# Early sums: stores and loads begun by ScalarE, three sum buffers, two weight buffers

## The chip, the cores and the metric

One core of one Trainium2 chip. The metric is device time in microseconds of one execution; three executions of the kernel before are known.

## The reference

Three layers follow each other. First a recurrence over 768 steps with a 40x40 state per head (4 batches of 8 heads). Its output is reshaped to 3072 tokens of 320 features. Then two feed-forward layers:

```
y[t] = r[t] @ state;  state = state * w[t] - (state @ a[t]) b[t]^T + v[t] k[t]^T
h = x @ w_in;  solu = h * softmax(h);  x = (layernorm(solu) * g_ln) @ w_out     # d_ff 1024
h = x @ w_in2; g = max(h, 0) + alpha * min(h, 0);  out = g @ w_out2             # d_ff 2048
```

## The kernel before

**Windows and slots.** The recurrence is cut into 12 windows of 64 steps; each window has two slots, so 24 slots, 0 to 23, run one after the other in `slot(g)`. A slot does the attention of 32 steps (`stage_x`, `stage_u`, `stage_uf`, `stage_st`, `stage_g2`, `stage_s`, `stage_y`) and, in between, pieces of work that lie in `queue`. Four slots share one triangular inverse (`inverse`, lines 368 and 372, 31 steps of VectorE), which is computed in the last two of the four slots before. TensorE runs in the order in which the program was written (`manual_schedule`). The other engines' instructions are put in order by the compiler's scheduler, by what it takes to be ready, and each engine then runs its own list strictly in order. SP (SyncE) begins all transfers, also strictly in order.

**The pieces in the queue.** `mlp_tasks(g)` fills it, in this order: the second transpose `ptx` of one token tile, then 16 products `mm1` of the first layer (line 589) with the transposes `ptr` (line 628) of another tile between them, then `soft` (the softmax pieces, lines 594 to 603, on VectorE, ScalarE and GpSimd), then the 8 steps of the second product `po` (lines 642 to 644). Normalising is line 606 on ScalarE. The tile for window w of the second layer's input is stored to `x2d` at line 663. `pace` and `wait` take pieces out of the queue to keep TensorE at work.

**The early sums.** The last layer's first product has 16 pieces f per window. For windows 1 to 8 the first 8 of them are computed ahead, in slots 9 to 23, as 64 units. A unit is four calls of `ahead_sums` (line 881, eight products of 128x256 in all) into the PSUM tile `ph1`. Then ScalarE copies the sum into the SBUF tile `hb` (line 884) and SP stores it to `hd` (line 886). It needs the weights `wr`, loaded from `whd` by `unit_load` (line 865) at the beginning of the unit two before, and the window's input `xw`, loaded by `window_load` (line 870) at the beginning of the window's first slot. Slots 9 to 22 have four units each, put after products 3, 7 and 16 and at the end of the queue; slot 23 has eight, the last five at the end of the queue.

**Buffers.** `hb` has one buffer, `xw` one, `wr` three. `ph1`, `ptr`, `po` and `ptx` share two PSUM buffers (pool `ps_w`).

**Other names that the steps touch.** VectorE's `lnl` (line 634) follows ScalarE's `lnh` (line 633) and frees `ptr`. `kbf` (line 244) and `XS` (line 254) are inputs of later windows, loaded by SP; GpSimd works on `XS` at line 326 and on `VUS` at line 499. Weights of the last layer are decoded from 64-bit words in the same slots (`raw`, `em`). After slot 23 a second phase does the last layer; there `hd` is read back.

Of the kernel before, what the change touches and what calls it, by code (L numbers as in the profile page):

```python
# [7 lines left out]
F32 = mybir.dt.float32  # L8
# [31 lines left out]
NI = 18  # L40
ZF = (1, 1, 1, 1)
WO, JW = 1, 2
NF, NR = 8, 3
UP = (3, 7, 16)
NH = 3
WF, WL = 1, 8
FLOOR2 = (4000, 1300)
U0 = 2 * WF + 7
# [6 lines left out]
def tile_kernel(ctx: ExitStack, tc: tile.TileContext, w_fm, a0_fm, a_fm, kb_fm, r_fm, v_fm, v_tm,  # L55
                w1_in, w1_out, g_ln, w2_in, w2_out, alpha, ident_d, mask_d, r, k, v, w, a, b, w1_nat, out,
                manual=True):
    nc = tc.nc
    NW = w_fm.shape[0]
    NG = 2 * NW  # L60
# [7 lines left out]
    def pool(stack, name, bufs, **kw):  # L68
        return stack.enter_context(tc.tile_pool(name=name, bufs=bufs, **kw))
# [13 lines left out]
    x2_d = [dr.tile([128, 5, 256], F32R, name=f"x2d{w}") for w in range(NW)]  # L83
# [5 lines left out]
    whd = [dr.tile([128, 2, 2, 3, 128], F32, name=f"whd{j}") for j in range(NF // 2)]  # L89
    hd = [[dr.tile([128, 512], F32, name=f"hd{w}_{f}") for f in range(NF)] for w in range(WF, WL + 1, 2)]  # L90

    cm = pool(ctx, "cm", 1)
    pm = ctx.enter_context(ExitStack())
    ps_h = pool(pm, "ps_h", 1, space=PSUM)
    ps_w = pool(pm, "ps_w", 2, space=PSUM)
    m1 = pool(pm, "m1", 1)
    m2 = pool(pm, "m2", 2)
    m3 = pool(pm, "m3", NR)
    b2 = pool(ctx, "b2", 2, side="right")
    lm = pool(ctx, "lm", 1, side="right")  # L100
    pa = ctx.enter_context(ExitStack())
# [25 lines left out]
    def f32(ap):  # L127
        return ap.bitcast(F32)
# [37 lines left out]
    st = {}  # L166
# [60 lines left out]
    def flush(n):  # L227
        while len(queue) > n:
            pop()
# [375 lines left out]
    def norm(P, m):  # L605
        nc.scalar.activation(out=P, in_=P, func=AF.Identity, scale=m[:, 8:9], bias=m[:, 9:10])
# [225 lines left out]
    def mlp_tasks(g):  # L832
        t1, t2 = g - 3, g - 4
        pt = PTR if g % 4 else PT0
        q = []
        us = slot_units(g)
        if 0 <= t2 - 1 < NG:
            q.append((0.33, 768, lambda: tr2(t2 - 1)))
        for p in range(17):
            if p == NP and 0 <= t2 < NG:  # L840
                q.append((0.0, 0, lambda: norm(st["P", t2], st["sm", t2])))
            if 0 <= t2 < NG:
                q += [(0.22, 512, lambda j=j: tr1(t2, j)) for j in range(4) if pt[j] == p]
            if 0 <= t1 < NG and p < 16:
                q.append((0.216, 512, lambda p=p: mm1(t1, p)))
            if p in UP and us:
                q += unit_tasks(us.pop(0))
        if 0 <= t1 < NG:
            q.append((0.0, 0, lambda: soft(t1)))
        if 0 <= t2 < NG:  # L850
            for p in range(K1):
                q.append((0.4, 960, lambda p=p: mm2(t2, p)))
        for i in us:
            q += unit_tasks(i)
        return q
# [2 lines left out]
    units = [(w, f) for w in range(WF, WL + 1) for f in range(NF)]  # L858
    loaded = []

    def unit_load():
        if len(loaded) < len(units):
            w, f = units[len(loaded)]
            t = m3.tile([128, 2, 3, 128], F32R, name="wr")
            nc.sync.dma_start(out=f32(t[:]), in_=whd[f // 2][:, f % 2])
            loaded.append(t)

    def window_load(w):
        st["xw"] = m1.tile([128, 5, 256], F32R, name="xw")
        nc.sync.dma_start(out=f32(st["xw"][:]), in_=f32(x2_d[w][:]))  # L870

    def ahead_sums(i, piece):
        w, f = units[i]
        if piece == 0:
            unit_load()
            st["ph"] = ps_w.tile([128, 512], F32, name="ph1", tag="w")[:, 0:256]
        wr, x, p = loaded[i], st["xw"], st["ph"]
        ops = [(wr[:, 0, 0], x[:, 0]), (wr[:, 0, 0], x[:, 1]), (wr[:, 1, 0], x[:, 0]), (wr[:, 0, 1], x[:, 2]),
               (wr[:, 0, 1], x[:, 3]), (wr[:, 1, 1], x[:, 2]), (wr[:, 0, 2], x[:, 4]), (wr[:, 1, 2], x[:, 4])]
        for j in range(2 * piece, 2 * piece + 2):  # L880
            nc.tensor.matmul(p, lhsT=ops[j][0], rhs=ops[j][1], start=j == 0, stop=j == 7)  # L881
        if piece == 3:
            hb = m1.tile([128, 256], F32, name="hb")
            nc.scalar.copy(out=hb, in_=p)  # L884
            c = (w - WF) % 2 * 256
            nc.sync.dma_start(out=hd[(w - WF) // 2][f][:, c:c + 256], in_=hb)

    def unit_tasks(i):
        return [(0.236, 512, lambda p=p: ahead_sums(i, p)) for p in range(4)]

    def slot_units(g):

        w, c = divmod(g - 7, 2)
        if not WF <= w <= WL:
            return []
        b = (w - WF) * NF
        if g == NG - 1:
            return list(range(b, b + NF))
        return list(range(b + c * NF // 2, b + (c + 1) * NF // 2))
# [22 lines left out]
    def slot(g):  # L922
        st["slot"] = g
        pre, late, at = fill_tasks(g)
        inv = inv_tasks(g)
        fin = g == NG - 1
        ni = len(inv)
        pos = [0]
        queue.extend(mlp_tasks(g))

        def dec(n=1):
            with tc.issue_after(st["fence"].ins):
                for _ in range(min(n, len(wts))):
                    wts.pop(0)()

        if g == NG - 2:
            at.setdefault("x", []).append(early_w)

        def filler(x):
            for f in at.get(x, ()):  # L940
                f()

        def invs(x):
            while pos[0] < ni and pos[0] < x * ni:
                inv[pos[0]]()
                pos[0] += 1

        if g + 1 < NG:
            load_g(g + 1)
        us = slot_units(g)  # L950
        if us and us[0] % NF == 0:
            window_load(WF + us[0] // NF)
            if us[0] == 0:
                for _ in range(NR - 1):
                    unit_load()
        stage_x(g)
        filler("a")
        with tc.issue_after(st["fence"].ins):
            for f in pre:
                f()  # L960
        filler("b")
        if g == 0:
            st["busy"] = st["idle"]
            keep(KEEP1)
        stage_u(g)
        nd = (ND if g < 4 else NL if g >= NG - 4 else NC)[g % 4]
        invs(0.2)
        stage_uf(g, 0)
        stage_uf(g, 1)
        filler("c")  # L970
        dec((nd + 3) // 4)
        invs(0.4)
        if not fin:
            stage_st(g, 0)
            stage_st(g, 1)
        invs(0.6)
        stage_g2(g, 0)
        dec((nd + 1) // 4)
        filler("x")
        filler("d")  # L980
        stage_g2(g, 1)
        invs(1.0)
        with tc.issue_after(st["fence"].ins):
            for f in late:
                f()
        filler("e")
        dec((nd + 2) // 4)
        if not fin:
            stage_s(g, 0)
            stage_s(g, 1)  # L990
        invs(1.0)
        dec(nd // 4)
        filler("f")
        flush(RES)
        stage_y(g)
        filler("z")
        flush(0)
        if g % 2 == 1 and not fin:
            x_move(g // 2)
# [462 lines left out]
```

## Time and profile before

| | |
|---|---|
| median of 3 executions | 1253.87 us (1252.38 to 1257.45) |
| profiled execution, its own time | 1249.18 us |
| span in the profile | 1247.4 us |
| mean granted TensorE clock | 0.879 |
| busy: TensorE / VectorE / ScalarE / GpSimd | 81% / 64% / 44% / 40% |
| slots 9 to 23 | about 390 to 917 us of the span |

In the rows, PE is TensorE's products and PEld its weight loads, DVE is VectorE, ACT ScalarE, POOL GpSimd, SP SyncE, and "SPq" SP's queue, which begins transfers. L884 is line 884 of the kernel. Times are microseconds from the start of the span, unless ns is said. A row of waits reads: engine, its line, whom it waited for, total us, times, longest. In rows in order of time, the bracket at the end tells how long the engine was idle before and what ended that. The issue of a transfer is not its movement: a row of SPq lasts as long as SP needs to begin it. PEclk is the granted clock as a share of 2.4 GHz. Idle time of an engine that isn't the bottleneck costs nothing.

### The profile page before, as it was taken

What the parts mean: (1) busy time and instruction counts of PE and PEld (TensorE: products, weight loads), DVE (VectorE), ACT (ScalarE), POOL (GpSimd) and SP (SyncE); (2) the same over time, 40 slices, a digit from 0 to 9 for tenths busy, and PEclk for the clock granted to TensorE, in tenths of its full rate; (3) what the DMA queues carried; (4) which work ended last, traced back from release to release, by engine and by line L of the source; (5) the groups of instructions that cost most, each with busy time, mean ns of one, the idle gap of its engine ahead of it and who ended that gap; (6) DMA issues with size and microseconds to landing.
All of it is one profiled execution on the core that took longest, in us unless ns stands there. A gap on an engine that the chain in (4) does not pass through costs nothing.

```text
span 1247.4 us, 38106 instructions
## 1 busy us (share of the span) xinstructions
PE 1008.0 (81%) x16197; PEld 841.3 (67%) x16197; DVE 794.3 (64%) x1610; ACT 544.3 (44%) x1268; POOL 501.3 (40%) x552
## 2 busy tenths in 40 slices
PE   7286676847786959697786877897888999999997
PEld 3144454736675757575675766776778999999997
DVE  8896899766985796467964686344346544444343
ACT  3335544555545625465454634554445322222221
POOL 6857545434353314233242322232215444444332
PEclk8586887778887978898788988998999999999999
DMA  6423343344444535464445555465374332330000
GB/s 169 121 63 99 97 116 101 103 115 115 111 129 128 165 99 155 146 181 136 127 129 164 144 165 153 137 205 172 118 214 165 92 105 58 108 115 30 22 19 17
DMA packets 139910, 149.93 MB, mean 120 GB/s; under 512 B 41428, under 2 KB 106580, under 8 KB 139732
## 3 DMA queue, kind: packets, MB, share of 16 engines
q1 hardware_dynamic: 139732, 147.42, 41.0%
q8 instruction: 129, 2.11, 0.7%
q14 instruction: 49, 0.40, 0.1%
HBM read 111.99 MB, written 35.39 MB: 118 GB/s over the span
## 4 chain that ended last, share of the span: by engine, by line
PE 40%; DVE 31%; DMA 9%; ACT 7%; issue 6%; POOL 5%; SPq 1%; POOLq 0%; DVEq 0%; ACTq 0%
PE ph L1126 9%; DVE tmp L368 6%; DVE LMN L372 5%; PE acc L1141 4%; PE acc L1139 4%; PE acc L1140 4%; PE h L589 3%; PE ph L881 2%; DVE VUS L496 2%; DMA raw<-in_w_in_dram 2%; DMA hd<-hb 2%; DMA kbf<-in_kb_fm_dram 2%; PE po L642 1%; DVE sm L594 1%; DVE kbf L317 1%
## 5 line engine op out<-in xcount | busy, mean ns | idle before, releaser
L1115 POOL TENSOR_TENSOR gll<-gt,gh 128x512 fp32r<-128x512 f32 (+1 forms) x112 | 126.9, 1144 | 174.1 <-ACT gh L1114 164.3
L1114 ACT CAST gh<-gt 128x512 fp32r<-128x512 f32 (+1 forms) x112 | 62.1, 560 | 199.8 <-DVE gt L610 188.1
L609 DVE TENSOR_SCALAR gt<-ph,al 128x512 f32<-128x512 f32 (+1 forms) x80 | 51.4, 643 | 145.4 <-PE ph L1126 145.2
L642 PE MATMUL po<-wo1h,lnh 128*128 128x320 f32 x192 | 73.1, 381 | 52.4 <-ACT hb L884 36.0
L881 PE MATMUL ph<-xw,wr 128*128 128x256 f32 x512 | 86.9, 302 | 22.5 <-DMA xw<-x2d 9.9
L589 PE MATMUL h<-w1h,xt 128*128 128x512 f32 x240 | 98.0, 461 | 0.0
L881 PEld LDWEIGHTS ph<-xw,wr 128*128 128x128 f32 x512 | 73.0, 197 | 33.1 <-issue 8.9
L368 DVE TENSOR_TENSOR tmp<-LMN,LMN 128x87 f32<-128x87 f32 (+25 forms) x189 | 90.1, 488 | 4.3
L1141 PE MATMUL acc<-w2h,gll 128*128 128x320 f32 x288 | 89.2, 310 | 0.0
L1139 PE MATMUL acc<-w2h,gh 128*128 128x320 f32 x288 | 89.1, 309 | 0.0
L1140 PE MATMUL acc<-w2l,gh 128*128 128x320 f32 x288 | 89.1, 309 | 0.0
L326 POOL TENSOR_TENSOR XS<-XS,H 40x512 f32<-40x512 f32 (+1 forms) x48 | 64.1, 1340 | 61.9 <-DMA XS<-in_a_fm_dram 34.0
L542 POOL TENSOR_TENSOR YS<-YS,mask 64x512 f32<-64x512 f32 x48 | 65.8, 1372 | 52.4 <-ACT YS L541 50.6
L225 PE MATMUL busy<-busy 128*128 128x512 bf16 x221 | 69.0, 469 | 20.0 <-DVE busy L1029 18.7
L642 PEld LDWEIGHTS po<-wo1h,lnh 128*128 128x128 f32 x192 | 43.3, 225 | 56.9 <-ACT hb L884 37.5
L679 POOL TENSOR_TENSOR dec<-em 128x256 f32<-128x256 f32 x36 | 28.7, 796 | 116.9 <-DVE em L676 73.5
L372 DVE TENSOR_TENSOR LMN<-LMN,tmp 128x87 f32<-128x87 f32 (+25 forms) x189 | 72.3, 394 | 3.4
L643 PE MATMUL po<-wo1l,lnh 128*128 128x320 f32 x192 | 67.2, 350 | 0.0
L644 PE MATMUL po<-wo1h,lnl 128*128 128x320 f32 x192 | 67.0, 349 | 0.0
L602 POOL TENSOR_TENSOR sm<-sm,half 128x1 f32<-128x1 f32 x24 | 15.6, 649 | 125.4 <-DVE sm L601 123.5
L589 PE MATMUL h<-w1l,xt 128*128 128x512 f32 x144 | 65.3, 454 | 0.0
L496 DVE TENSOR_TENSOR VUS<-pst,VUS 40x320 f32<-40x320 f32 x92 | 44.9, 488 | 29.4 <-PE pst L491 27.4
(205 smaller groups left out, 2816.7 us busy)
## 6 DMA issues: line engine op xcount, KB each, us to landing
wr<-whd SPq DMA_DIRECT2D x64, 384.0 KB
kbf<-in_kb_fm_dram SPq DMA_DIRECT2D x24, 416.0 KB
hd<-hb SPq DMA_DIRECT2D x64, 128.0 KB
hl<-hd SPq DMA_DIRECT2D x32, 256.0 KB
x2d<-x SPq DMA_DIRECT2D x24, 320.0 KB
xd<-Y SPq DMA_DIRECT2D x24, 256.0 KB
xt<-xd SPq DMA_DIRECT2D x12, 512.0 KB
raw<-in_w_in_dram SPq DMA_DIRECT2D x20, 256.0 KB
```

Source lines behind the costliest of these rows:

```text
L225: nc.tensor.matmul(st["busy"], lhsT=busy[:, 0:128], rhs=busy, start=True, stop=True)
L368: eng.tensor_tensor(out=tv[:, a - rows[0][0]:b - rows[0][0]], in0=M[:, a:b, s:s + 1].to_broadcast(sh), in1=l.unsqueeze(1).to_broadcast(sh) ...
L372: r = eng.tensor_tensor(out=o, in0=o, in1=tv[:, a - rows[0][0]:b - rows[0][0]], op=ALU.add)
L496: st["fence"] = nc.vector.tensor_tensor(out=d, in0=p_[o:o + 40], in1=v[o:o + 40, e, sl, :], op=ALU.add)
L589: nc.tensor.matmul(st["h"][:, ns], lhsT=l, rhs=r, start=j == 0, stop=j == len(ops) - 1)
L642: nc.tensor.matmul(po, lhsT=lh[:, k], rhs=wo1h[:, k], start=k == 0, stop=False)
L881: nc.tensor.matmul(p, lhsT=ops[j][0], rhs=ops[j][1], start=j == 0, stop=j == 7)
L1115: nc.gpsimd.tensor_tensor(out=gll, in0=t, in1=f32(gh), op=ALU.subtract)
L1126: nc.tensor.matmul(p, lhsT=l, rhs=r, start=j == 0, stop=j == len(ops) - 1)
L1139: nc.tensor.matmul(acc, lhsT=gh[:, cs], rhs=oh, start=first, stop=False)
L1140: nc.tensor.matmul(acc, lhsT=gh[:, cs], rhs=ol, start=False, stop=False)
L1141: nc.tensor.matmul(acc, lhsT=gll[:, cs], rhs=oh, start=False, stop=last)
```

## The change

ScalarE, not SP, begins the store of a sum, right behind its copy, then the load of the weights for the unit two later, and behind a window's last unit the load of the next window's input. `hb` gets three buffers (pool `mb`), `wr` two instead of three. The first window and the first two weight loads stay on SP, at the beginning of slot 9 (U0). In slot 23 the units go after products 1, 3, 5, 7, 10, 13 and 16, and one stays at the end.

```
-NF, NR = 8, 3
-UP = (3, 7, 16)
+NF, NR, NB = 8, 2, 3
+UP, UPL = (3, 7, 16), (1, 3, 5, 7, 10, 13, 16)
...
+    mb = pool(pm, "mb", NB)
...
-            if p in UP and us:
+            if p in (UP if g < NG - 1 else UPL) and us:
                 q += unit_tasks(us.pop(0))
...
-    def unit_load():
+    def unit_load(eng):
...
-            nc.sync.dma_start(out=f32(t[:]), in_=whd[f // 2][:, f % 2])
+            eng.dma_start(out=f32(t[:]), in_=whd[f // 2][:, f % 2])
             loaded.append(t)
 
-    def window_load(w):
+    def window_load(w, eng):
         st["xw"] = m1.tile([128, 5, 256], F32R, name="xw")
-        nc.sync.dma_start(out=f32(st["xw"][:]), in_=f32(x2_d[w][:]))
+        eng.dma_start(out=f32(st["xw"][:]), in_=f32(x2_d[w][:]))
...
         if piece == 0:
-            unit_load()
...
         if piece == 3:
-            hb = m1.tile([128, 256], F32, name="hb")
+            hb = mb.tile([128, 256], F32, name="hb")
             nc.scalar.copy(out=hb, in_=p)
             c = (w - WF) % 2 * 256
-            nc.sync.dma_start(out=hd[(w - WF) // 2][f][:, c:c + 256], in_=hb)
+            nc.scalar.dma_start(out=hd[(w - WF) // 2][f][:, c:c + 256], in_=hb)
+            unit_load(nc.scalar)
+            if f == NF - 1 and w < WL:
+                window_load(w + 1, nc.scalar)
...
-        us = slot_units(g)
-        if us and us[0] % NF == 0:
-            window_load(WF + us[0] // NF)
-            if us[0] == 0:
-                for _ in range(NR - 1):
-                    unit_load()
+        if g == U0:
+            window_load(WF, nc.sync)
+            for _ in range(NR):
+                unit_load(nc.sync)
         stage_x(g)
```

## Rows read from the trace of the kernel before

**Rows 1.** Windows: us of each stretch, busy us and instructions of each engine.
```profile
core 0: us, PE busy (x) PEld busy (x) DVE busy (x) ACT busy (x) POOL busy (x), PEclk, DMA share, GB/s
...
425.00:460.00 35.00, 23.93 (x448) 20.18 (x448) 29.90 (x65) 13.70 (x31) 5.29 (x8) 0.80 0.46 131
...
496.00:531.00 35.00, 25.41 (x581) 21.80 (x576) 16.82 (x32) 15.73 (x38) 8.35 (x11) 0.85 0.47 138
...
785.00:819.00 34.00, 29.07 (x646) 24.73 (x640) 12.69 (x29) 15.85 (x37) 9.26 (x12) 0.90 0.49 145
...
844.00:880.00 36.00, 28.92 (x602) 24.05 (x602) 15.66 (x37) 15.81 (x36) 9.23 (x13) 0.86 0.49 150
880.00:917.00 37.00, 30.57 (x473) 25.73 (x471) 9.55 (x22) 15.39 (x37) 6.61 (x7) 0.95 0.45 139
```

**Rows 2.** Waits of TensorE, 390 to 917 us: total us, times, longest.
```profile
PE po L642 <- ACT hb L884: 36.0, 7, 7.0
PE ptr L628 <- DVE lnl L634: 12.2, 9, 1.9
...
PE ph L881 <- DVE lnl L634: 4.5, 4, 2.0
...
PE ph L881 <- DMA wr<-whd: 3.7, 1, 3.7
PE ph L881 <- ACT hb L884: 2.6, 2, 1.5
```

**Rows 3.** Chain that ended last, slot 12: start us, us, what.
```profile
518.95 1.24 ACT P L606
520.18 0.27 ACT hb L884
```

**Rows 4.** In order of time, slots 10 and 12: SP, ScalarE, TensorE.
```profile
508.41 0.48 SPq L886 DMA_DIRECT2D hd<-hb  x1
...
520.09 0.35 ACT L884 COPY hb<-ph 128x256 f32<-128x256 f32 x1
...
446.19 0.64 PE L642 MATMUL po<-wo1h,lnh 128*128 128x320 f32 x1 [6.24 <-ACT hb L884]
...
520.49 0.63 PE L642 MATMUL po<-wo1h,lnh 128*128 128x320 f32 x1 [6.63 <-ACT hb L884]
```

**Rows 5.** Chain that ended last, slot 10.
```profile
446.09 0.62 DVE tmp L368
```

**Rows 6.** Waits of SP's queue, whole span.
```profile
SPq L886 <- ACT hb L884: 135.2, 39, 12.9
```

**Rows 7.** Chain that ended last, slot 11.
```profile
476.62 0.37 ACT hb L884
...
477.39 0.54 SPq L244
...
477.98 4.03 DMA XS<-in_a_fm_dram
...
482.08 1.33 POOL XS L326
```

**Rows 8.** Tiles hb and wr: ns shortest/median/longest, first and last start us.
```profile
L884 ACT COPY hb<-ph x64: 348/372/377, 396.9 to 916.5; 128x256 f32<-128x256 f32 x64
L886 SPq DMA_DIRECT2D hd<-hb x64: 319/337/611, 397.3 to 916.9; - x64
...
L865 SPq DMA_DIRECT2D wr<-whd x64: 319/389/1252, 276.2 to 905.2; - x64
```

**Rows 9.** In order of time, beginning of slot 23: SP, then TensorE.
```profile
880.46 0.32 SPq L870 DMA_DIRECT2D xw<-x2d  x1
...
884.50 1.19 PE L881 MATMUL ph<-xw,wr 128*128 128x256 f32 x8 [1.94 <-DMA xw<-x2d]
```

**Rows 10.** The page's chain by line, shares of the span.
```profile
PE ph L1126 9%; DVE tmp L368 6%; DVE LMN L372 5%; PE acc L1141 4%; PE acc L1139 4%; PE acc L1140 4%; PE h L589 3%; PE ph L881 2%; DVE VUS L496 2%; DMA raw<-in_w_in_dram 2%; DMA hd<-hb 2%; DMA kbf<-in_kb_fm_dram 2%; PE po L642 1%; DVE sm L594 1%; DVE kbf L317 1%
```

## The prediction

> **What bounds the kernel now.** I read the windows first, to see which slots leave TensorE idle; then TensorE's waits, for what the idle time is; then the chain and the instructions in order of time at one wait of each kind, for whether it sets the end; last SP's waits and the durations of the pieces that move.
>
> The change lives in slots 9 to 23 (390 to 917 us). The windows [rows 1] show two kinds of slot. In slot 10 (425 to 460) VectorE is busy 29.9 us of 35 and TensorE 23.9: the 31-step inverse sets the time. In slots 12, 20, 22 and 23 TensorE is the busiest engine and still idle for 9.6, 4.9, 7.1 and 6.4 us; VectorE has 16.8 us or less there.
>
> The waits [rows 2] name the idle time. The largest is the second product (`po`, line 642), which waited for the copy of an early sum (`hb`, line 884): 36.0 us in 7 times. The transposes (`ptr`) waited 12.2 us and the sums' own products 4.5 us for `lnl`: `ph1`, `ptr` and `po` share two PSUM buffers, and with one held by a sum that isn't copied, the rest turns in a single buffer.
>
> Does that set the end? In slot 12 it does: on the chain [rows 3] normalising (line 606) ends, the copy follows at 520.18, and the product starts. In order of time [rows 4] `po` stood idle 6.63 us; the copy ran at 520.09 and the store ahead of it left SP only at 508.41. So the copy stands in ScalarE's program behind the softmax pieces, as something that has one SBUF buffer and a store on a busy queue. In slot 10 a like wait ended at 446.19 after 6.24 us [rows 4], but there the chain is on the inverse [rows 5].
>
> SP suffers too: its stores stood 135.2 us waiting for copies [rows 6], with everything behind them in line. In slot 11 that is on the chain [rows 7]: the copy at 476.62 lets the store go, behind it a load of `kbf`, then the load of `XS` (4.03 us), which GpSimd needs.
>
> **The change part by part.** It moves 133 issues from SP to ScalarE: 64 stores, 62 weight loads and 7 window loads (the first two weight loads and the first window stay on SP). It gives `hb` two more buffers, takes one from `wr`, and spreads slot 23's units.
>
> *Copies that no longer wait, TensorE-bound slots.* With three buffers a copy waits on the store of three units ago, and can stand right behind its unit in ScalarE's program. Slot 12: of 9.6 us idle I take back 7.5, the 6.63 and one transpose wait of about 1.3 (12.2/9), less a little for the next limit, the softmax chain on VectorE and ScalarE. Slot 16 repeats slot 12: 15 together. Slot 20: 3.5 of 4.9. Slot 22: 5.5 of 7.1, because its 3.71 us wait for `wr` [rows 2] was a load late on SP. Sum 24; bounds 7 (half of the 6.63 in slots 12 and 16, nothing in 20 and 22) and 31.2 (all idle time of the four).
>
> *Copies in the inverse's slots (10, 14, 18).* Three of the seven waits. Nothing, since VectorE covers them; if that cover were gone, some 6 us each.
>
> *SP's line.* Slots 11 and 15: `XS` and `kbf` loads no longer stand behind a store. The mean stand is 135.2/39 = 3.5 us; GpSimd also needs the recurrence of the slot, so I take 2 each: 4, bounds 0 and 7.
>
> *The issues on ScalarE.* No row shows a DMA issued by ScalarE. The nearest are SP's: 0.337 us for a store, 0.389 for a weight load at the median, 1.252 at the longest [rows 8], 0.32 for a window load [rows 9]. All 133 come to 21.6 + 24.1 + 2.2 = 48 us of ScalarE. Most lies beside other work; what counts is where ScalarE's next instruction is on the chain. Following the chain I count ten units of the 64 with that (the starts of three inverses, the two fourth slots as in [rows 7], the rest around the softmax pieces). Each pays 0.73 for two issues: -7.5. Bounds 0 (it can be no gain) and 10 x 2 x 1.252 = -25. I take the medians, since the moved queue carries only these transfers.
>
> *The window load* came at 880.46, as the last product of the old window ended, and the first sum used it at 884.50, 4.04 us later, after 1.94 us of waiting [rows 9]. Now the copy (0.372), the store and the weight load go first: 1.1 us later at each of seven window ends. Four or so have slack; I take -2 for the seven outside slot 23, bounds 0 and -7.7.
>
> *Two weight buffers.* A load now starts after the copy of the unit before last, and has one unit and the products between to land; a landing takes under the window load's 4.04 us (384 against 640 KB). In slots 9 to 22 units lie mostly that far apart. Nothing; without that cover, 1 to 2 us in each of 14 slots.
>
> *Slot 23.* Idle 6.4 us. The chain gives the stores there most of its 2% [rows 10], but TensorE itself waited for copies only 2.6 us [rows 2]; the rest of the stretch is busy. Spreading the eight units (after products 1, 3, 5, 7, 10, 13, 16) removes the row of copies at its end. Against that the first unit stands two products earlier (about 0.5 us) and its window is 1.1 us later, and units two products apart wait for the two weight buffers. I take +3, bounds -4 and +6.4.
>
> Two short transpose waits on copies I leave at nothing. **Sum:** 24 + 4 - 7.5 - 2 + 3 = 21.5 gained. The profiled execution took 1249.18 us (span 1247.4), 4.7 below the median 1253.87. Taken from that execution: 1227.7; from the median: 1232, which I give.
>
> **Two rules weighed.** The rows say that 135.2 us of waiting in SP's line goes with the stores, and that the copies wait for places, not bytes. The Trainium skill ("DMA: Bandwidth & Descriptors", "Issuing engines are not separate DMA queues") says that transfers from any engine share the same 16 DMA engines, and another issuer saves only sequencer time, usually small. By that alone, nothing on the chain would change and the time would stay at 1254; the rows of waits speak against, as the sequencer's time here includes its waits.
>
> For the price of an issue the rows have 0.32 to 1.25 us on SP alone. The Trainium skill ("Perfetto Trace Analysis", "DMA Instruction — HWDGE (DVE, Sync)") says that a sequencer locks the descriptor generator for itself, so that ScalarE could stand behind an issue of SP. With one SP store more ahead of each, the ScalarE term would by that page be an estimated -14 instead of -7.5. No run here shows it yet.
>
> **The rivals.**
> 1. *More comes back.* After an idle stretch TensorE is granted 1.2 GHz instead of 2.4 for a while (mean 0.85 of the full clock in slot 12, 0.95 in slot 23 [rows 1]); with all idle time of slots 12, 16, 20 and 22 back and issues that hide: 31 + 7 + 3 - 2 = 39, so 1215. For it: SP's line is freed everywhere. Against: the softmax chain is close behind. Chance 0.19.
> 2. *No change.* ScalarE's order isn't made by `hb` but by the softmax pieces, so the copies stay late, or transfers cost as before and the sums wait for `wr` in its two buffers (14 slots x 1.5 = 21, against 21.5). 1248 to 1260, say 1253. For it: chains through VectorE's inverse in six slots don't move. Against: [rows 4], where the store stood until 508.41. Chance 0.12.
> 3. *Slower.* ScalarE's queue becomes the bound, in the TensorE-bound slots, where VUS, XP and softmax copies stand behind two issues. The gains without its term are 29. With units on the chain, 60 issues of the 133, it decides from 0.48 us an issue, between the median and the longest of [rows 8]; at 0.8 it gives -48, so 19 slower: 1273. Against: only ten units now have ScalarE next on the chain. Chance 0.08.
>
> **How the numbers follow.** My forecast, 1232, has 0.61. A measurement of this kernel can tell some 0.5%, 6.3 us. The forecast and rival 1 lie below 1247.6 (0.80, nearly all of both); rival 2 gives 0.12 within 0.5%; rival 3 gives 0.08. The low end, 1211, takes all idle time with a free ScalarE and slot 23's 2.6; the high end, 1250, takes the gains' low bounds (7 + 0) with part of the costs, and reaches into rival 2. Left out are rival 3, part of rival 2, and a gain over 43.
>
> **What the changed profile would show.** Right: `po` waiting for `hb` falls from 36.0 us to under 8; copies within about 2 us of their unit's last product; no SP wait at the store's line; slots 12 and 16 shorter by 6 to 8 us each; slots 10, 14 and 18 of the same length; 133 issues on ScalarE of 0.3 to 0.5 us. The window load leaves about 1 us later behind its last product. Wrong, if ScalarE's issues take over 0.5 us with the chain running through them, if the copies still stand behind line 606, or if the sums' waits for `wr` or `xw` exceed 20 us.

## The result and the profile after

The median fell from 1253.12 us (4 executions, 1251.63 to 1257.45) to 1204.86 us (4, 1201.25 to 1208.51): ratio 0.9609, 95% interval 0.9570 to 0.9649. The gain is 48 us; 21.5 were forecast, and the range ended at 1211. The profiled execution took 1203.22 us, its span 1201.4 us, 46.0 less than before. Kernel lines 99 to 874 of before stand one further down.

Where the 46.0 us lie is read from the windows. Kernel before, slots 9 to 23, what follows them (the second phase), and slots 10, 20 and 22 in full (columns as in [rows 1]):

```profile
386.60:913.10 526.50, 421.53 (x8673) 353.79 (x8673) 318.33 (x673) 261.50 (x633) 154.04 (x184) 0.87 0.51 151
913.10:1247.40 334.30, 321.65 (x1985) 300.07 (x1983) 153.66 (x272) 96.83 (x185) 138.73 (x123) 0.99 0.28 84
420.20:466.10 45.90, 30.69 (x546) 25.21 (x544) 39.58 (x88) 18.71 (x44) 10.61 (x16) 0.83 0.45 133
...
786.30:818.40 32.10, 27.17 (x546) 23.01 (x545) 12.18 (x29) 14.35 (x33) 8.12 (x11) 0.89 0.51 152
846.30:880.40 34.10, 27.02 (x539) 22.39 (x541) 13.52 (x30) 14.93 (x33) 8.57 (x12) 0.85 0.48 151
```

Kernel after, the same two stretches, then slots 10, 20 and 22:

```profile
387.50:870.80 483.30, 412.63 (x8675) 346.15 (x8674) 318.70 (x676) 261.40 (x636) 159.19 (x184) 0.90 0.59 166
870.80:1201.40 330.60, 320.95 (x1985) 299.93 (x1982) 152.58 (x272) 96.70 (x185) 137.47 (x123) 0.99 0.29 85
...
421.60:454.40 32.80, 28.20 (x554) 23.17 (x548) 26.20 (x56) 18.14 (x42) 11.01 (x15) 0.90 0.57 156
...
755.00:779.50 24.50, 24.00 (x545) 20.42 (x544) 11.98 (x28) 13.62 (x31) 7.79 (x10) 1.00 0.69 205
810.30:836.70 26.40, 23.58 (x536) 19.50 (x536) 11.70 (x28) 14.68 (x32) 7.17 (x10) 1.00 0.59 181
```

Slots 9 to 23 gave 43.2 us and the second phase 3.7; the stretch ahead of slot 9 took 0.9 more. TensorE's idle time in the slots fell from 105.0 us (526.5 less 421.5) to 70.7; its busy time fell by another 8.9, since the granted clock rose from 0.87 to 0.90. By slot, each measured from its first `px` product to that of the next (us):

| slots | before | after | gain | forecast |
|---|---|---|---|---|
| 10 + 11 | 45.9 + 31.6 | 32.8 + 33.4 | 11.3 | 2 |
| 14 + 15 | 43.1 + 32.2 | 32.1 + 37.7 | 5.5 | 2 |
| 18 + 19 | 43.5 + 27.2 | 30.0 + 35.2 | 5.5 | 0 |
| 12, 16 | 41.2, 40.9 | 41.4, 34.5 | -0.2, 6.4 | 7.5, 7.5 |
| 20, 22 | 32.1, 34.0 | 24.5, 26.4 | 7.6, 7.6 | 3.5, 5.5 |
| 23, second phase | 32.8, 334.3 | 34.1, 330.6 | -1.3, 3.7 | 3 |

A single slot of one execution is not firm. The run below with slot 23's units at their old places has the same order of instructions on VectorE, ScalarE and GpSimd, and of transfers on SP and ScalarE, up to slot 23, so it repeats these slots: there 10 + 11 took 71.0, 14 + 15 66.7, 18 + 19 63.1, slots 12 and 16 34.3 and 33.2, slots 20 and 22 24.5 and 27.9. Slot 12 alone differs by 7.1 us, the three pairs together by 0.4 (201.2 and 200.8).

Half of the gain, 22.3 us, came from slots 10, 14 and 18 with the slot behind each, where 4 us were forecast. The inverse of 62 VectorE instructions is not quicker: it ended 50.4 us after the start of slot 10 in before, 53.0 us in after, and TensorE asks for its result only in slot 12 (`pu`), 32.9 and 26.1 us later. Its last instruction and the first product that reads it, before and then after:

```profile
468.48 2.10 DVE L401 STREAM_TRANSPOSE LMN<-LMN 128x1024 f32<-128x1024 f32 x1
...
503.50 0.79 PE L456 MATMUL pu<-XP,LMN 32*32 32x40 f32 x64
```

```profile
472.44 2.17 DVE L402 STREAM_TRANSPOSE LMN<-LMN 128x1024 f32<-128x1024 f32 x1
...
500.69 0.91 PE L457 MATMUL pu<-XP,LMN 32*32 32x40 f32 x64
```

What moved is the place of the recurrence's own VectorE steps in its list. VectorE and then TensorE in slot 10 of before, in order of time (start, us, engine, line; the bracket is idle time and what ended it):

```profile
452.61 0.99 DVE L496 TENSOR_TENSOR VUS<-pst,VUS 40x320 f32<-40x320 f32 x2
...
459.25 2.01 DVE L522 TENSOR_TENSOR KBS<-pss,KBS 40x320 f32<-40x320 f32 x4
...
464.49 0.68 DVE L558 TENSOR_TENSOR Yt<-py,H 104x512 f32<-104x512 f32 x1
```

```profile
453.75 1.29 PE L514 MATMUL pss<-KBS,VUS 64*40 64x40 f32 x32 [2.81 <-DVE VUS L496]
465.22 0.95 PE L415 MATMUL pt<-ident,kbf 104*128 104x104 f32 x4 [3.52 <-DVE Yt L558]
```

VectorE in slot 10 of after:

```profile
441.49 2.02 DVE L497 TENSOR_TENSOR VUS<-pst,VUS 40x320 f32<-40x320 f32 x4
...
447.34 0.49 DVE L523 TENSOR_TENSOR KBS<-pss,KBS 40x320 f32<-40x320 f32 x1
...
453.13 0.68 DVE L559 TENSOR_TENSOR Yt<-py,H 104x512 f32<-104x512 f32 x1
```

Before, the state add (`VUS`) starts 32.4 us into the slot, behind 36 of the inverse's 62 instructions, the key add (`KBS`) behind 45 and the output product (`Yt`) behind 53. After, the add starts 19.9 us into the slot, behind 14, the others behind 18 and 24. The rest of the inverse then runs in slot 11, which fits that 11, 15 and 19 became longer. The compiler's scheduler wrote both lists. In the trace of before the adds aren't the largest wait yet: of the 15.2 us that TensorE stood idle in slot 10, `po` stood 6.24 for the copy [rows 4], and the two rows above 2.81 and 3.52. With the wait for the copy gone, the first experiment shows how far they hold TensorE.

TensorE's waits after, 385 to 890 us (total us, times, longest):

```profile
PE ph L881 <- DMA xw<-x2d: 12.0, 3, 6.4
PE ph L881 <- ACT KBS L420: 9.2, 2, 4.7
...
PE ph L881 <- ACT hb L884: 5.3, 2, 5.1
PE ph L881 <- issue: 4.3, 1, 4.3
...
PE po L643 <- ACT hb L884: 0.9, 2, 0.5
PE ph L881 <- DMA wr<-whd: 0.9, 2, 0.4
```

The 36.0 us of `po` [rows 2] are down to 0.9, and SP's 135.2 [rows 6] are gone with the stores. The copies come early: half of them start within 0.12 us of their unit's last product (2.24 in before), the latest after 7.0 us (17.4). What grew are the waits for a window's inputs. The profile puts 12.0 us to them, against 9.9 in before:

```profile
PE ph L881 <- DMA xw<-x2d: 9.9, 3, 4.9
```

But the two waits put down to `KBS` and the 4.3 us put down to "issue" are also first units of a window. Ahead of the first units of the seven windows whose loads were moved, TensorE stood idle for 5.0 us in sum before the change and 23.3 us after it. The end of one window's last product, ScalarE's queue (ACTq) and the next window's first product:

```profile
451.61 0.48 PE L881 MATMUL ph<-xw,wr 128*128 128x256 f32 x2
...
456.23 0.39 ACTq L871 DMA_DIRECT2D xw<-x2d  x1
...
461.76 1.20 PE L881 MATMUL ph<-xw,wr 128*128 128x256 f32 x4 [4.45 <-ACT KBS L420]
```

The load starts 4.1 us behind the last product's end: it stands behind the copy in ScalarE's list, and the copy came at 455.40, 3.3 us behind. From the issue to the product 5.5 us pass. The `KBS` copy named ended 0.9 us before the product, is nothing that it reads, and frees no buffer of it; so I take the input for what came last. Over the seven windows the load starts 1.3 to 6.2 us behind the last product, 3.8 in the mean. And one copy still comes late, in slot 12, on the chain that ended last:

```profile
493.20 0.03 ACT P L607
...
494.94 0.28 ACT hb L884
...
495.26 2.08 PE ph L881 x8
```

Normalising (line 607) still stands ahead of it in ScalarE's list; the next unit's product, not `po`, stood 5.1 us for the copy. That is most of what slot 12 lost against slot 16, where this wait is 0.2 us. In the run that repeats these slots it is 1.2 us, with the same list.

The moved pieces themselves (ns shortest/median/longest, first and last start):

```profile
L886 ACTq DMA_DIRECT2D hd<-hb x64: 326/374/1842, 395.6 to 871.1; - x64
...
L866 ACTq DMA_DIRECT2D wr<-whd x62: 326/326/1387, 395.2 to 861.7; - x62
...
L871 ACTq DMA_DIRECT2D xw<-x2d x7: 389/442/1185, 456.2 to 838.1; - x7
```

### The profile page after: what moved, and what is told of

The parts are those of the page before. It is cut to its first block, busy times and chain, and to the rows that moved or that the text cites. A ratio compares the mean times of both kernels' runs of the same rounds, so it can differ in the third digit from the quotient of the medians.

```text
span 1201.4 us, 38118 instructions
## 1 busy us (share of the span) xinstructions
PE 993.6 (83%) x16197; PEld 829.7 (69%) x16197; DVE 793.3 (66%) x1610; ACT 543.3 (45%) x1268; POOL 505.3 (42%) x552
## 3 DMA queue, kind: packets, MB, share of 16 engines
q1 hardware_dynamic: 120580, 110.06, 32.9%
## 4 chain that ended last, share of the span: by engine, by line
PE 41%; DVE 31%; DMA 8%; ACT 7%; POOL 6%; issue 5%; SPq 1%; ACTq 0%; DVEq 0%; POOLq 0%
PE ph L1127 10%; DVE tmp L369 5%; PE acc L1142 5%; PE acc L1140 5%; PE acc L1141 5%; DVE LMN L373 4%; PE h L590 4%; PE ph L881 3%; DMA kbf<-in_kb_fm_dram 2%; DVE VUS L497 2%; DMA raw<-in_w_in_dram 2%; DVE H L292 2%; DVE F L296 2%; DVE KBS L523 1%; DVE sm L595 1%
## 5 line engine op out<-in xcount | busy, mean ns | idle before, releaser
L881 PE MATMUL ph<-xw,wr 128*128 128x256 f32 x512 | 93.9, 318 | 38.3 <-DMA xw<-x2d 12.0
L881 PEld LDWEIGHTS ph<-xw,wr 128*128 128x128 f32 x512 | 79.0, 213 | 50.9 <-ACT KBS L420 13.6
L369 DVE TENSOR_TENSOR tmp<-LMN,LMN 128x87 f32<-128x87 f32 (+25 forms) x189 | 93.2, 505 | 4.2
L643 PE MATMUL po<-wo1h,lnh 128*128 128x320 f32 x192 | 67.2, 350 | 18.0 <-DVE lnl L635 17.0
L373 DVE TENSOR_TENSOR LMN<-LMN,tmp 128x87 f32<-128x87 f32 (+25 forms) x189 | 70.7, 385 | 3.4
L644 PE MATMUL po<-wo1l,lnh 128*128 128x320 f32 x192 | 62.9, 328 | 0.0
L645 PE MATMUL po<-wo1h,lnl 128*128 128x320 f32 x192 | 62.6, 326 | 0.0
L226 PEld LDWEIGHTS <-busy 128*128 128x128 bf16 x221 | 23.4, 114 | 53.3 <-DVE busy L1030 20.6
L555 PEld LDWEIGHTS py<-YS,KBS 128*40 128x40 f32 (+1 forms) x1536 | 37.0, 135 | 32.6 <-POOL XS L327 13.3
L351 DVE TENSOR_TENSOR XS<-pg,mask 32x256 f32<-32x256 f32 x96 | 39.8, 414 | 28.7 <-ACT LMN L354 22.8
```

Source lines behind the costliest of these rows:

```text
L226: nc.tensor.matmul(st["busy"], lhsT=busy[:, 0:128], rhs=busy, start=True, stop=True)
L369: eng.tensor_tensor(out=tv[:, a - rows[0][0]:b - rows[0][0]], in0=M[:, a:b, s:s + 1].to_broadcast(sh), in1=l.unsqueeze(1).to_broadcast(sh) ...
L373: r = eng.tensor_tensor(out=o, in0=o, in1=tv[:, a - rows[0][0]:b - rows[0][0]], op=ALU.add)
L643: nc.tensor.matmul(po, lhsT=lh[:, k], rhs=wo1h[:, k], start=k == 0, stop=False)
```

## The experiments

Two questions: which part of the change makes the gain (buffers, stores or loads), and by which road it shortens slots 10, 14 and 18: by VectorE's list, or by loads that are late on the chip whatever the list. The kernel before took 1252.8 to 1254.0 us in these comparisons. The quoted texts were written before each run. In six of the fourteen runs (one sum buffer; all three held; the two with the adds first and all on SP; stores alone; order of ScalarE alone) the time fell between the ranges of the theories weighed, which fits several causes at work.

**Everything back on SP, new buffers kept** (after, edited):

```
-            nc.scalar.dma_start(out=hd[(w - WF) // 2][f][:, c:c + 256], in_=hb)
-            unit_load(nc.scalar)
+            nc.sync.dma_start(out=hd[(w - WF) // 2][f][:, c:c + 256], in_=hb)
+            unit_load(nc.sync)
             if f == NF - 1 and w < WL:
-                window_load(w + 1, nc.scalar)
+                window_load(w + 1, nc.sync)
```

> The changed kernel with all 133 issues back on SP; three sum buffers, two weight buffers and the new places in slot 23 stay. Theory A (the issuer matters: in SP's line stores and loads stand behind other transfers, so the schedule has the copies late and puts the recurrence's VectorE adds of slots 10, 14 and 18 behind the inverse's middle, 41 of some 60 inverse instructions in the written order, against 13 in the changed kernel): 1240 to 1265 us, slots 10, 14 and 18 of 42 us or more. Theory B (the prediction's: the buffers free the copies): 1205 to 1220 us, TensorE's wait of po for hb under 8 us.

1245.7 us, ratio 0.993 (0.990 to 0.996). All but the issuer is worth 8 us together: three sum buffers, two weight buffers, the spreading, and the loads' new place in the program behind the store, which this run keeps. No run has three sum buffers and three weight buffers at once. The profiled execution took 1238.6 us, the shortest of six; slots 12 and 16 have their shorter time (35.3 each), slots 10, 14 and 18 are longer than before (50.3, 46.1, 45.7). TensorE's and SP's waits, 385 to 890 us:

```profile
PE pss L515 <- DVE VUS L497: 31.0, 3, 12.5
PE ph L881 <- DMA wr<-whd: 16.2, 7, 3.8
PE ph L881 <- DMA xw<-x2d: 13.8, 4, 6.0
```

```profile
SPq L886 <- ACT hb L884: 54.7, 26, 5.8
SPq L866 <- PE ph L881: 50.5, 23, 5.6
```

TensorE stands 31.0 us for the state adds, once in each of the three slots: the wait of `po` for `hb` is gone, and the one behind it came out. SP still stands at the stores and at the weight loads, and everything behind them in its line stands too.

**One sum buffer, issued by ScalarE** (after, edited):

```
-NF, NR, NB = 8, 2, 3
+NF, NR, NB = 8, 2, 1
```

> The changed kernel with one sum buffer instead of three. Theory A (issuer): 1200 to 1215 us, since a store begun right behind its copy is done before the next unit's copy; the adds stand at 13 of 60 in the written order as in the changed kernel. Theory B (buffers): copies wait for the store of the unit before as in the kernel before (35.6 us in 18 times there), 1230 to 1254 us.

1217.4 us, 0.970 (0.967 to 0.973). Slots 10, 14 and 18 are short (31.0, 29.2, 29.3), slots 12 and 16 as long as before (42.0, 41.7). The issuer shortens the inverse's slots; the three sum buffers are worth 12.5 us on top.

**The state adds held behind the inverse** (after; the slots' part of the inverse is handed out ahead, and `VUS` queued behind its last step):

```
+            with tc.issue_after(st["hold"].ins) if g in (10, 14, 18) else ExitStack():
-            st["fence"] = nc.vector.tensor_tensor(out=d, in0=p_[o:o + 40], in1=v[o:o + 40, e, sl, :], op=ALU.add)
+                st["fence"] = nc.vector.tensor_tensor(out=d, in0=p_[o:o + 40], in1=v[o:o + 40, e, sl, :], op=ALU.add)
...
-        invs(0.4)
+        invs(1.0 if g in (10, 14, 18) else 0.4)
+        st["hold"] = st["step"]
```

> The changed kernel with the recurrence's four VectorE adds (line 497) of slots 10, 14 and 18 queued behind step 16 of the inverse, about where the kernel before had them. Theory A (their place among the inverse's steps cost the time of those slots; the inverse itself is due only two slots later): 15 to 25 us slower, 1220 to 1230 us. Rival C (the inverse's length sets those slots and the time came from TensorE's shorter stalls): within 6 us of the changed kernel, 1199 to 1211 us.

1205.9 us, 0.960 (0.957 to 0.963): no change, a miss for the order theory as tried here. The time lies in the rival's range. The adds did come late (453.27 us in slot 10), but `KBS` and `Yt` stayed in front of them. By the code, the sum is needed only by the next slot, and `pss` reads nothing that the add writes; its wait in before is then one for a PSUM buffer that the add frees. Here the second `pss` stood 1.54 us for the copy of `YS` instead. So the test that decides has to hold all three.

**All three held** (the same edit, and besides):

```
+                with tc.issue_after(st["hold"].ins) if g in (10, 14, 18) else ExitStack():
                     nc.vector.tensor_tensor(out=d, in0=p_[o:o + 40], in1=k[o:o + 40, 1 - e, sl, :], op=ALU.add)
...
+        with tc.issue_after(st["hold"].ins) if g in (10, 14, 18) else ExitStack():
             nc.vector.tensor_tensor(out=Yt, in0=py[0:104], in1=st[w]["H"][:, :, ts], op=ALU.mult)
```

> The kernel after with all three of the recurrence's VectorE steps (state add, key add, output product) of slots 10, 14 and 18 queued behind the part of the inverse done in these slots, 34 of its instructions; issues stay on ScalarE. The two runs that put them first gained 9 us each. If the order by itself is worth that much or more: 1212 to 1225 us. If only the order together with SP's late line costs: 1200 to 1210 us. If the order were the whole of it: 1235 us or more.

1227.3 us, 0.979 (0.973 to 0.984): 22 us more than after, with ScalarE still issuing. TensorE's waits (lines shifted by the edit):

```profile
PE py L466 <- DVE VUS L498: 13.9, 3, 5.6
...
PE py L466 <- DVE KBS L525: 7.2, 2, 3.7
```

Slots 10, 14 and 18 with the slot behind each are longer by 8.1 us in sum; 11.0 of the rest lie in slot 16 and 4.0 in slot 22, which the hold isn't meant for. So 22 us are not the price of the order alone: the hold also changes what the scheduler puts around it.

**The reverse: adds first, everything on SP**, then the same edit on the kernel before:

```
-        invs(0.6)
+        with tc.issue_after(st["fence"].ins) if g in (10, 14, 18) else ExitStack():
+            invs(0.6)
...
-        invs(1.0)
+        with tc.issue_after(st["fence"].ins) if g in (10, 14, 18) else ExitStack():
+            invs(1.0)
```

> The kernel with every issue on SP but the new buffers (1245.7 us), and in slots 10, 14 and 18 the inverse's later steps are queued behind the recurrence's adds on VectorE, as they stand in the kernel after. Theory (what ScalarE's issuing gains is the order on VectorE: with SP's line the adds stand behind two thirds of the inverse and TensorE waits 31.0 us for them in these slots): 1215 to 1225 us, slots 10, 14 and 18 some 10 us shorter each, and the wait of TensorE's state products for the adds gone. Rival (SP's line itself is late on the chip: stores and loads queued behind other moves; the order is a by-product): 1238 to 1250 us, with the same time waited for weights or inputs.

> The kernel before, nothing changed but that in slots 10, 14 and 18 the inverse's later steps are queued behind the recurrence's adds on VectorE. Theory (the order on VectorE is what makes these slots long): 1228 to 1242 us, slots 10, 14 and 18 shorter by 5 to 12 us each, part of it given back in 11, 15 and 19 where the rest of the inverse then lies. Rival (the slots are long because of the copies and stores, and the order follows from that): 1250 to 1256 us, no change.

1236.4 us, 0.988 (0.984 to 0.992), and 1245.2 us, 0.994 (0.991 to 0.997): 9 us each, a third of what the first text wanted and half of the second's. The first interval overlaps that of the same kernel without the edit (0.990 to 0.996) a little; the second lies clear of 1. Slots 10, 14 and 18 with the slot behind each are shorter by 14.9 and 12.4 us in sum, but slots 12 and 16 together longer by 9.3 and 7.2. In the first, the 31.0 us for `VUS` went, and other waits grew in their place:

```profile
PE ph L881 <- DMA wr<-whd: 23.6, 7, 8.0
PE ph L881 <- DMA xw<-x2d: 12.8, 5, 6.9
...
PE pss L515 <- DVE VUS L497: 2.0, 2, 1.0
```

In slots 12 and 16 of that run the longest wait of each is one for weights, 4.7 and 8.0 us. So the order is one part; the loads are a second one behind it. In the kernel before, with three weight buffers, the second limit was `po` with 29.0 us for `hb`.

**Stores alone, then loads alone on ScalarE** (after; the first edit, then the second instead):

```
-            unit_load(nc.scalar)
+            unit_load(nc.sync)
             if f == NF - 1 and w < WL:
-                window_load(w + 1, nc.scalar)
+                window_load(w + 1, nc.sync)
```

```
-            nc.scalar.dma_start(out=hd[(w - WF) // 2][f][:, c:c + 256], in_=hb)
+            nc.sync.dma_start(out=hd[(w - WF) // 2][f][:, c:c + 256], in_=hb)
```

> The kernel after with the loads of weights and windows put back on SP; only the stores stay on ScalarE. In its written order on VectorE the recurrence's adds of slots 10, 14 and 18 stand behind 35 to 48 of the inverse's 62 instructions, as with everything on SP. Theory (the loads behind the x moves in SP's line are what costs, on the chip by waits for weights and inputs, and through the order): 1230 to 1248 us, near the kernel with everything on SP (1245.7 us), with waits of TensorE for weights or inputs. Rival (the stores are what held SP's line): 1200 to 1215 us.

> The kernel after with the stores put back on SP; the loads of weights and windows stay on ScalarE. The adds keep their early places in VectorE's order (behind 11 to 13 inverse instructions). Theory (the loads are what matters): 1200 to 1215 us, and as 64 issues go from ScalarE perhaps a few us below the kernel after. Rival (the stores): 1230 to 1248 us, with TensorE or ScalarE waiting for a sum buffer.

1225.4 us, 0.976 (0.973 to 0.980), between the two ranges, and 1197.0 us, 0.953 (0.949 to 0.957), 3 us below the theory's range. All four cases together, with three sum buffers and two weight buffers in each:

| | loads by SP | loads by ScalarE |
|---|---|---|
| stores by SP | 1245.7 | 1197.0 |
| stores by ScalarE | 1225.4 | 1204.9 |

Moving the loads gains 48.7 us with the stores on SP and 20.5 with them on ScalarE; moving the stores gains 20.3 without the loads and costs 7.9 with them. The scheduler's list goes with the loads: the state add of slot 10 stands behind 42 of the inverse's instructions with everything on SP, 35 with the stores alone on ScalarE, 12 with the loads alone, 14 with both. With the loads gone, SP's standing at the stores costs nothing that these times show; the first row is SP's wait, the second TensorE's, with loads on ScalarE alone:

```profile
SPq L886 <- ACT hb L884: 81.9, 31, 9.0
```

```profile
PE ph L881 <- DMA xw<-x2d: 2.6, 1, 2.6
```

With the stores gone instead, SP stood at the weight loads themselves, for the products that free one of the two weight buffers:

```profile
SPq L866 <- PE ph L881: 55.5, 26, 7.3
```

**Stores on ScalarE, loads on SP, adds first** (the first of these two edits, with the one that queues `invs` behind the adds):

> Stores on ScalarE, loads of weights and windows on SP (1225.4 us as it is), and in slots 10, 14 and 18 the inverse's later steps queued behind the recurrence's adds on VectorE, as in the kernel after. The kernel after with the adds made late took 1227.3 us, 22 us more. If the loads on SP cost only through this order: 1203 to 1212 us, and the waits of TensorE for weights and inputs stay under 13 us in sum. If they are late on the chip whatever the order: 1216 to 1228 us, the waits for weights and inputs (28.1 us with the adds late) at 28 us or more, in place of the waits for the adds (24.8 us).

1217.1 us, 0.971 (0.969 to 0.974). TensorE's waits with the adds late, then with the adds first:

```profile
PE pss L515 <- DVE VUS L497: 24.8, 3, 11.1
PE ph L881 <- DMA wr<-whd: 16.8, 8, 5.5
PE ph L881 <- DMA xw<-x2d: 11.3, 3, 5.9
```

```profile
PE ph L881 <- DMA wr<-whd: 35.8, 10, 8.0
PE ph L881 <- DMA xw<-x2d: 11.0, 3, 6.1
```

Of the 20.5 us between the stores alone on ScalarE (1225.4 us) and the change, the order gives 8.3 at the medians (the intervals overlap between 0.973 and 0.974); 12.2 stay with the loads, and the waits for the adds turned into waits for weights (16.8 to 35.8 us). With two weight buffers the loads on SP are late on the chip under both of VectorE's lists. Slots 12 and 16 are longer by 12.6 us in sum here too, and slots 10, 14 and 18 with the slot behind each shorter by 22.1.

**The price of an issue** (after, the store as two halves, 64 issues more):

```
-            nc.scalar.dma_start(out=hd[(w - WF) // 2][f][:, c:c + 256], in_=hb)
+            for h in (0, 128):
+                nc.scalar.dma_start(out=hd[(w - WF) // 2][f][:, c + h:c + h + 128], in_=hb[:, h:h + 128])
```

> The kernel after with each sum's store issued as two halves: 64 issues more on ScalarE, the same bytes. The prediction took 0.73 us for ten issues as the price of an issue; the trace after shows 0.326 to 0.374 us median for one. If an issue lies on the path in full: 64 x 0.35 = 22 us, 1227 us. If ScalarE has room, as the prediction's small term and the waits of ScalarE for TensorE (34.4 us in 27) say: 1203 to 1212 us.

1209.7 us, 0.966 (0.962 to 0.970): 4.8 us for 64 issues, 0.08 us each, with intervals that overlap. The 22 us of issues in full are ruled out; most of an issue hides.

**Order of ScalarE alone** (before; `soft` queued behind the last copy):

```
+    def soft_behind(t):
+        with tc.issue_after(st["copied"].ins) if "copied" in st else ExitStack():
+            soft(t)
...
-            q.append((0.0, 0, lambda: soft(t1)))
+            q.append((0.0, 0, lambda: soft_behind(t1)))
...
-            nc.scalar.copy(out=hb, in_=p)
+            st["copied"] = nc.scalar.copy(out=hb, in_=p)
```

> The kernel before with one edit: ScalarE's softmax pieces are queued behind the copy of the unit ahead of them; one sum buffer, all issues on SP. If ScalarE's order alone made the stalls of po (rows 3 and 4): their 36.0 us fall under 10 and the time to 1215 to 1235 us. Theory A (the cause lies in SP's line, ScalarE's order only follows it): softmax waits for the late copy instead, 1245 to 1265 us.

1239.8 us, 0.989 (0.984 to 0.994). The waits of `po` for `hb` went altogether, and the first text's time didn't follow: 21.9 us of waits for `VUS` came in their place (4.7 in before). Slots 12 and 16 fell by 5 to 7 us (36.0, 34.2) with one sum buffer, all on SP; slots 10, 14 and 18 stayed long (41.7, 49.1, 44.4), and slot 23 rose to 37.7. So the forecast's mechanism for 12 and 16 exists, but it is the small part.

**Slot 23's units at their old places** (after, edited):

```
-UP, UPL = (3, 7, 16), (1, 3, 5, 7, 10, 13, 16)
+UP, UPL = (3, 7, 16), (3, 7, 16)
```

> The kernel after with the units of the last slot (23) put back at three places instead of seven. If the spreading is worth what the prediction gave it or more (0 to 8 us, all of it in slot 23, whose length in the kernel after is 34.1 us): 1205 to 1213 us, slot 23 longer. If the spreading costs, since the first unit is asked for sooner than its window arrives (6.4 us wait at 844.84 in slot 22/23): 1198 to 1205 us, slot 23 shorter. All slots before 23 as in the kernel after by either.

1208.9 us, 0.966 (0.959 to 0.973). Slot 23 is 43.0 us instead of 34.1, slots 10 to 22 are shorter by 2.4 in sum though their order is the same; the spreading is worth 4 us at the medians, not told apart from nothing by the intervals.

**The window in three tiles** (after; each loaded by ScalarE as soon as the last unit has used it):

```
-    def window_load(w, eng):
-        st["xw"] = m1.tile([128, 5, 256], F32R, name="xw")
-        eng.dma_start(out=f32(st["xw"][:]), in_=f32(x2_d[w][:]))
+    def window_load(w, eng, part):
+        k, n = ((0, 2), (2, 2), (4, 1))[part]
+        t = m1.tile([128, n, 256], F32R, name=f"xw{part}")
+        eng.dma_start(out=f32(t[:]), in_=f32(x2_d[w][:, k:k + n]))
...
+        if piece and f == NF - 1 and w < WL:
+            window_load(w + 1, nc.scalar, piece - 1)
```

> The kernel after keeps one buffer for the window's five input blocks, and TensorE stood about 25 us in it before the first unit of a new window (4.45 us at 461.76, 4.71 at 787.50, 6.40 at 844.84 and four more). Here the five blocks are three tiles, each loaded again as soon as the last unit of the window has used it, so a load starts up to one unit's steps sooner. If these waits lie on the path that sets the end: 1185 to 1197 us, and the waits before a window's first unit fall to under 10 us in sum. If another chain (VectorE's adds and inverse, ScalarE's line) ends as late: 1200 to 1210 us, with the waits gone and other waits in their place. ScalarE issues 14 DMAs more; if an issue costs its median 0.35 us on the path, that is 5 us of it.

1192.1 us, 0.954 (0.947 to 0.962), as the theory had it. Ahead of the first units of the seven windows TensorE stood idle for 0.2 us instead of 23.3; the waits put down to inputs fell from 12.0 us to

```profile
PE ph L886 <- DMA xw<-x2d: 3.3, 4, 1.9
```

The lowest median of all, though its interval overlaps that of the change.

**Both edits that beat the change** (the edit for three tiles, and the store on `nc.sync` as above):

> The two edits that each beat the kernel after put together: the window's inputs in three tiles, loaded by ScalarE as they come free (1192.1 us), and the stores back on SP (1197.0 us). If they add up (12.8 and 7.9 us off 1204.9 us): 1180 to 1187 us. If both had taken away the same waits for the first unit of a window (12.0 us for inputs in the kernel after, 2.6 us with the stores alone put back): 1188 to 1197 us.

1196.7 us, 0.955 (0.949 to 0.960): they don't add up. The text's reason isn't it: the 2.6 us with the stores alone put back belong to the first window, which SP loads. Ahead of the first units of the other seven TensorE stood 12.8 us there, put down to other things, and not at all here, yet the time is the same: slots 12 and 16 took 42.0 and 43.1 us instead of 32.4 and 37.2. Why, no run shows. The three versions under 1200 us can't be told apart; only the one with the stores alone put back has an interval (0.9493 to 0.9568) that ends below where that of the change begins (0.9570).

## Why the prediction was wrong

**The step that failed** is the term of the copies in the inverse's slots (10, 14, 18), put at "Nothing, since VectorE covers them". With the slot behind each, these slots gave 22.3 us, and with the term of SP's line 4 were forecast. VectorE was busy and the chain ran through the inverse [rows 5], both read rightly. But the inverse was due only two slots later, 33 us after its end. What held TensorE in these slots was the late copy and, behind it, the place of three short steps of the recurrence in VectorE's list. That list is the scheduler's: with the loads by ScalarE it stands otherwise. I took a list for a limit. Where the wait of `po` went and the loads stayed on SP (everything on SP; order of ScalarE alone), these slots with the slot behind each were 8.7 and 6.8 us longer in sum than in before. Putting the adds first took 12 to 22 us off them, 8 to 9 net (three times, at the medians). The rest goes with the loads: with ScalarE as their issuer, 12.2 us more than the adds first give.

**The second part of the same miss** is the 4 us for SP's line. I counted `XS` and `kbf` behind the stores, but not the weight and window loads, which the change takes out of that line. In the trace of before, with three weight buffers, TensorE waited 3.7 us for weights [rows 2]; with two it waits as soon as the loads are on SP: 16.2 us with everything there, 35.8 us with only the loads there and the adds early. That the third buffer hid their lateness is my reading; the loads' place in the program moved as well, and no run parts the two. "Nothing" for two weight buffers was right with ScalarE as issuer (0.9 us in two waits).

**Slots 12 and 16: 15 forecast; 6.2 in the profiled execution, 14.6 in the run that repeats these slots.** So the size was about right. The mechanism was so in part: most copies came early, but in slot 12 the copy still stands behind normalising, as rival 2 had it, at 5.1 us in one execution and 1.2 in the other. With all on SP the two slots take 35.3 us each.

**Slots 20 and 22: 9 forecast, 15.2 measured.** Idle time gave 4.4 and 4.3 of it (from 4.9 to 0.5 and from 7.1 to 2.8). The rest is TensorE's busy time, which fell from 27.17 us to 24.00 and from 27.02 to 23.58, at a granted clock of 1.00, the upper of its two levels (2.4 GHz), instead of 0.89 and 0.85. Rival 1 named this mechanism; it stopped at the idle time.

**ScalarE's issues: 7.5 forecast** (ten times 0.73 is 7.3). No run prices all 133. The two that bear on 64 each give a like size: moving the stores to ScalarE costs 7.9 us net where the loads are there already, doubling them 4.8. Their medians, 0.326 to 0.374 us, are near SP's 0.337 and 0.389 [rows 8]; the longest, 1.842 us, is above SP's 0.611 for the store. Rival 3, ScalarE as the bound, didn't come.

**The window load: 2 forecast.** Too small. I had it 1.1 us later, by the lengths of copy, store and weight load; but the copy itself comes late at most window ends, and the load starts 3.8 us behind the last product in the mean. TensorE's idle time before the first units rose by 18.3 us (5.0 to 23.3). Splitting the load, which also lets it start before the last unit ends, gains 12.8 us at the medians.

**Slot 23: 3 forecast; 2.4 measured** over slot 23 and the second phase together (-1.3 and 3.7); the second phase's part is no effect of the spreading that any run shows.

**The range's low end, 1211**, was to take all idle time, a free ScalarE and slot 23's 2.6 us; these terms come to 40.8 us, so 1213. The measured gain lies beyond, since two things aren't in it: the inverse's slots, and busy time that shrinks with the clock.

**The signs named.** Met: `po` under 8 us, 54 of the 64 copies within 2 us of their product, issues of 0.3 to 0.5 us at the median. Not met: slots 10, 14 and 18 of the same length. Of the signs of being wrong two came: a copy behind normalising (slot 12), and, if first units count as waits for inputs, more than 20 us of those.

**The two rules.** By the first (the Trainium skill, "DMA: Bandwidth & Descriptors", "Issuing engines are not separate DMA queues") the time would have stayed at 1254. The runs disagree: the same loads begun by ScalarE rather than SP take 48.7 us off with the stores on SP, 20.5 with them on ScalarE. What counts is how long the issuer's line stands, and what lists the scheduler writes for the engines. The second (the Trainium skill, "Perfetto Trace Analysis", "DMA Instruction — HWDGE (DVE, Sync)") led to an estimate of -14 for ScalarE's issues; the 0.08 us of an extra issue and the 7.9 us of the stores speak for less, and no run shows a lock by itself.

**Open:** how the 41 us between everything on SP and the change part between the order and the late loads. Adds put first give 8 to 9 us net, adds put late cost 22, of which 8.1 lie in the slots meant; each hold makes the scheduler write other lists. A run with the same lists and only another issuer wasn't tried, nor one with three weight buffers and the loads on SP.

## What to carry to other kernels

When an engine is busy and on the chain, look at when its result is due before calling it the limit: if long work with slack stands ahead of short work without, the order is what costs, and any edit that shifts what the scheduler holds for ready can change it. Loads that must be early don't belong in an in-order line where other transfers wait for late results; here taking the loads out of that line paid, and the stores could stay. Where a change removes a buffer of a load, price the load as if bare: the waits in the trace are those with the buffer. And before reading a few us from one slot, look at an execution that repeats it with the same lists: here one slot differed by 7 us.

## What the hardware showed that I had not expected

ScalarE begins a transfer while one of its own instructions runs. In slot 12 of after, ScalarE and ScalarE's queue in order of time:

```profile
493.20 1.24 ACT L607 ACTIVATE P<-P,sm 128x1024 f32<-128x1024 f32 x1 [4.58 <-POOL sm L604]
493.26 0.33 ACTq L866 DMA_DIRECT2D wr<-whd  x1
```

The weight load's issue, 493.26 to 493.59, lies within the 1.24 us of one instruction. That fits the low price of an issue, 0.08 us.

The second phase, which the edits don't touch, took 329.4 to 332.0 us in all nine profiles with the stores on ScalarE and 333.2 to 335.5 us in the seven with them on SP, the kernel before among them. The cause wasn't looked for.
